# The bounds of a second weight matrix by absolute passes instead of matmuls, in a planned attention and MLP kernel whose order and engine choices are drawn anew

## The chip, the cores and the metric

The kernel runs on one core of one Trainium2 chip. The metric is the device time of one execution in microseconds, as the median of several runs. The engines are TensorE (PE, with its weight loads as PEld), VectorE (DVE), ScalarE (ACT), GpSimd (POOL) and SyncE (SP), whose queue issues all transfers.

## The reference

The kernel computes causal attention for 4 images of 12 heads, 448 positions and 64 values each, and puts the result through a dense layer, h - tanh(h), and a second dense layer.

```python
scores = scale * np.matmul(q, k.transpose(0, 1, 3, 2))
scores = np.where(mask, -1000000000.0, scores)
scores = scores - np.max(scores, axis=-1, keepdims=True)
attn = np.exp(scores)
attn = attn / (np.sum(attn, axis=-1, keepdims=True) + 1e-09)
x = np.matmul(attn, v)          # then to (4 * 448, 768)
h = x @ w_in                    # w_in: 768 x 2048, float64
out = (h - np.tanh(h)) @ w_out  # w_out: 2048 x 768, float64
```

## The kernel before

**Numbers.** Dense products run in float16 with each operand as a pair of a high and a low part, scaled by a power of two that comes from a bound on its absolute values; `split` (the high part by `scaled`, the low part on VectorE or GpSimd) makes the pairs, and a product takes three matmuls per block. The weights come as 64-bit floats. `decode` turns them into 32-bit ones: a pass on any of three engines picks three bits (the "shift" choice, written to a scratch in `e`), and for each half ScalarE scales the upper words into a PSUM bank and VectorE ors both together.

**Stages.** `first_rows` computes the first 128 positions of two images at a time in plain float32 (chunk `c` for images 0 and 1, `c2` for 2 and 3): scores, exponentials, transposes, a copy of the transposed weights out of PSUM (`pt`), and the products with v, all transposes and products through the one bank b_x. `w_in_chunk` loads, decodes, bounds and splits one eighth of w_in (8 times, two loads each). `mlp_g_first` runs the first layer for `c` and `c2`: 36 matmuls per eighth into one of the two banks b_m, a tanh on ScalarE, h - tanh on VectorE, and a split of the result. `w_out_half` loads and decodes w_out in 16 pieces of 256 rows by 384 columns, 8 per half, bounds each piece, takes the scale of the half and splits. `mlp2` is the second layer. Then `attention` runs over the four images for the other 320 positions: `prep` bounds and splits k, q and v, `weights_unit` and `weights_last` make the softmax weights and split them, a transposing transfer turns them, `values` multiplies with v and `split_x` stores x; `mlp_g` and `mlp2` follow per image. SBUF is shared over time: the g of `c` lies where the first rows were, and the pieces of w_out where w_in was decoded.

**The bounds of w_in and w_out.** `magnitudes` multiplies the two 16-bit halves of the words of a weight block in TensorE, with the block as its own stationary operand, so that the diagonal of the result holds sums of products that bound the magnitudes; 12 matmuls of 128 columns for an eighth of w_in, 6 for a piece of w_out, into the shared bank b_scales. VectorE reduces the bank, a matmul against an identity (`over_partitions`) spreads the result over the partitions, and `root_scale` takes the power of two. For q, k and v `bound` takes the largest absolute value directly: VectorE's reduction, or ScalarE's Abs with an accumulator; `bound_scale` then makes the scale.

**The order.** Nothing is written in program order. `Work.add` records each operation with its dependencies and a rank from the table RANK, `either` records alternatives on two or three engines and takes one by a letter of CFG (A, V or G), `cost` gives a duration, and `schedule` walks through a model of the engines: on the engine that is free first it takes, of the operations that are ready (or will be within AHEAD), the one of lowest rank. `emit` issues all operations by start time, so each engine has a fixed order of instructions and waits in it by semaphores. All instructions are issued by `emit`, hence one line, L288 (L302 after the change), for all.

Of the kernel before, what the change touches and what calls it, by code (L numbers as in the profile page):

```python
# [9 lines left out]
F32 = mybir.dt.float32  # L10
# [6 lines left out]
ALU = mybir.AluOpType  # L17
# [3 lines left out]
P = 128  # L21
# [4 lines left out]
class Work:  # L26
# [4 lines left out]
    LAT = {"A": 34.0, "V": 32.0, "G": 98.0, "T": 52.0, "S": 26.0}  # L31
    NEXT = {"A": 100.0, "V": 82.0, "G": 22.0}
    TURN = 94.0, 24.0
# [80 lines left out]
    def cost(self, eng, method, outs, ins):  # L114
# [11 lines left out]
        if eng == "T":  # L126
            f32 = ins[0].dtype == F32
            if method == "transpose":
                return 111.0, 170.0 if f32 else 166.0, None
            k, m = ins[0].shape[0], ins[0].shape[-1]  # L130
            quarter = ins[0].offset // ins[0].ap[0][0] if k <= 64 else None, o.offset // o.ap[0][0] if m <= 64 else None
            return (107.0 * n / P, 170.0, None) if f32 else (max(n / 2.4 + 2.5, 28.0), 166.0, quarter if min(k, m) <= 64 else None)
        if eng == "S":
            if "transpose" in method:
                c = o.size() / P
                return "turn", 1000.0 + 0.39 * c, c * 1.46
            store = o.space == bass.MemoryType.DRAM
            run = min(x.ap[-1][1] for x in ins + [o]) * size
            return ("store" if store else "load"), 450.0 if store else 440.0, o.size() * size / (360.0 if run >= 2048 else 235.0 if run >= 1024 else 385.0 if run >= 512 else 190.0)
# [14 lines left out]
        if method in ("tensor_scalar", "tensor_copy") and not psum and o.space != PSUM:  # L154
            if n < 16:
                return 142 + 5 * (n > 1) + 2.5 * n * (n > 2) + (50 if n == 1 else 65) * aps, n > 1
            return n * 0.52 + (150 if method == "tensor_copy" else 147) + 60 * aps, True
# [30 lines left out]
    def schedule(self):  # L188
# [12 lines left out]
        moved, since, last, warm, mode = 0.0, 0.0, 0.0, False, (True, True)  # L201
# [11 lines left out]
        while len(order) < n:  # L213
            t, e = min((next_at(e), e) for e in engines if ready[e] or waiting[e] or half is not None and half[1] == e)
# [3 lines left out]
            else:  # L218
# [3 lines left out]
                _, i = heapq.heappop(ready[e])  # L222
                if e == "T" and mode not in ((True, True), self.ops[i]["mode"]):
# [14 lines left out]
            if e == "T":  # L238
                turn = 0.0
                if o["mode"] != mode:  # L240
                    t, mode = max(t, free[e] + self.TURN[0]), o["mode"]
                    turn = self.TURN[1] * (mode != (True, True))
# [4 lines left out]
                warm = warm or t - since > 3100.0  # L247
                free[e] = last = t + (self.on_array(parts) + turn) * (1 if warm else 2)
                end = last + parts[-1][1] * (1 if warm else 1.15)
            elif e == "S":  # L250
                kind, issue, move = parts[0]
                moved = max(moved, t + (675.0 if kind == "turn" else 1300.0)) + move * (1.25 if t < 4500.0 else 1.0)
                free[e] = max(t + issue, moved - 2800.0)
                end = moved + {"turn": 885.0, "load": 1040.0, "store": 55.0}[kind]
            else:
# [6 lines left out]
                if part + 1 < len(parts):  # L262
                    o["start"] = t
                    free[e] = end + self.LAT[e]
# [50 lines left out]
def attention_then_mlp(ctx, tc, first, qk, v, w_in, w_out, out):  # L315
# [235 lines left out]
    def w_out_half(n):  # L551
# [4 lines left out]
        for m in range(4):  # L556
            for a in range(2):
# [405 lines left out]
```

## Time and profile before

| | us |
|---|---|
| median of 3 runs | 581.06 |
| lowest, highest | 581.05, 581.48 |
| the profiled execution | 579.8 |
| its span | 578.1 |

The span runs from the first to the last instruction; the execution's own time has 1.7 us around it. The granted clock of TensorE is 1.00 over the span. In all rows a group is named by what it writes and reads (`b_m<-slot,g`: from a weight slot and g into a bank b_m), with buffer numbers left out; `small` are the scalars per partition. An idle time in brackets or at a row's end stands with what ended it.

### The profile page before, as it was taken

What the parts mean: (1) busy time and instruction counts of PE and PEld (TensorE: products, weight loads), DVE (VectorE), ACT (ScalarE), POOL (GpSimd) and SP (SyncE); (2) the same over time, 40 slices, a digit from 0 to 9 for tenths busy, and PEclk for the clock granted to TensorE, in tenths of its full rate; (3) what the DMA queues carried; (4) which work ended last, traced back from release to release, by engine and by line L of the source; (5) the groups of instructions that cost most, each with busy time, mean ns of one, the idle gap of its engine ahead of it and who ended that gap; (6) DMA issues with size and microseconds to landing.
All of it is one profiled execution on the core that took longest, in us unless ns stands there. A gap on an engine that the chain in (4) does not pass through costs nothing.

```text
span 578.1 us, 13879 instructions
## 1 busy us (share of the span) xinstructions
PE 557.8 (96%) x5296; PEld 382.2 (66%) x5296; DVE 426.5 (74%) x1207; ACT 286.5 (50%) x751; POOL 341.9 (59%) x428
## 2 busy tenths in 40 slices
PE   6789999999999999999999999999999999999997
PEld 4567888866565666766666766566776566776664
DVE  5899999989999999699969996958599382332000
ACT  6899785744766845562555341606445150332000
POOL 3548965633563878975887888487956930542000
PEclk9999999999999999999999999999999999999999
DMA  8998379835486774365544435946123354000100
GB/s 305 343 298 310 112 213 258 239 110 178 102 161 136 183 163 78 93 174 124 119 118 92 92 66 109 211 100 125 42 69 62 69 80 101 2 1 1 28 28 27
DMA packets 109283, 74.04 MB, mean 128 GB/s; under 512 B 89760, under 2 KB 93344, under 8 KB 108704
## 3 DMA queue, kind: packets, MB, share of 16 engines
q1 hardware_dynamic: 109216, 73.15, 49.7%
q8 instruction: 41, 0.67, 0.5%
q14 instruction: 26, 0.21, 0.1%
HBM read 45.61 MB, written 5.51 MB: 88 GB/s over the span
## 4 chain that ended last, share of the span: by engine, by line
PE 68%; DVE 14%; DMA 7%; POOL 4%; issue 3%; ACT 2%; SPq 1%; DVEq 0%; POOLq 0%; ACTq 0%
PE b_m L288 57%; PE b_x L288 5%; PE b_s L288 5%; DVE pn L288 3%; DVE slot L288 2%; DVE small L288 2%; DVE prob L288 1%; PE b_scales L288 1%; DMA e<-in_v_dram 1%; DMA slot<-in_first_dram 1%; DMA g<-in_first_dram 1%; DVE g L288 1%; DVE first L288 1%; POOL first L288 1%; DMA pt<-pn 1%
## 5 line engine op out<-in xcount | busy, mean ns | idle before, releaser
L288 PE MATMUL b_m<-x,w_in 128*128 128x320 f16 (+1 forms) x1728 | 229.6, 290 | 1.6 <-DVE small L288 1.0
L288 PEld LDWEIGHTS <-w_in 128*128 128x128 f16 x1728 | 165.9, 98 | 56.3 <-issue 7.8
L288 PE MATMUL b_m<-slot,g 128*128 128x384 f16 x1152 | 191.7, 326 | 0.6 <-DVE t L288 0.5
L288 PEld LDWEIGHTS <-g 128*128 128x128 f16 x1152 | 111.1, 98 | 76.5 <-issue 5.1
L288 ACT ACTIVATE prob<-prob,small 128x256 f32<-128x256 f32 (+2 forms) x102 | 58.5, 574 | 62.2 <-DVE small L288 62.2
L288 ACT ACTIVATE t<-b_m,small 128x320 f32<-128x320 f32 (+1 forms) x70 | 37.6, 537 | 63.1 <-PE b_m L288 56.0
L288 DVE SCALAR_TENSOR_TENSOR t<-b_m,small,t 128x320 f32<-128x320 f32 (+1 forms) x70 | 39.4, 564 | 30.9 <-ACT t L288 30.7
L288 DVE CUSTOM_DVE_ANT_0 prob<-b_s,mask,small 128x384 f32<-128x384 f32 (+1 forms) x87 | 44.9, 549 | 8.6 <-PE b_s L288 7.5
L288 DVE TENSOR_SCALAR small<-small 128x1 f32<-128x1 f32 (+5 forms) x190 | 43.4, 242 | 6.1 <-ACT o L288 5.2
L288 ACT ACTIVATE o<-b_m,small 128x384 f32<-128x384 f32 x21 | 12.0, 572 | 61.3 <-PE b_m L288 61.3
L288 POOL TENSOR_SCALAR prob<-prob,small 128x384 f32<-128x384 f32 (+2 forms) x46 | 29.2, 634 | 18.9 <-ACT pn L288 6.6
L288 POOL TENSOR_SCALAR t<-t,small 128x320 f32<-128x320 f32 (+1 forms) x41 | 25.6, 625 | 23.9 <-ACT g L288 12.3
L288 POOL TENSOR_TENSOR g<-t,g 128x320 f16<-128x320 f32 (+1 forms) x40 | 34.1, 852 | 3.3
L288 PEld LDWEIGHTS <-v 128*64 128x64 f16 x1296 | 31.1, 111 | 7.1 <-issue 7.1
L288 DVE SCALAR_TENSOR_TENSOR pn<-prob,small,pn 128x256 f16<-128x256 f32 (+2 forms) x45 | 33.7, 767 | 1.5 <-ACT pn L288 0.8
L288 DVE SCALAR_TENSOR_TENSOR slot<-b_s,e 128x384 int32<-128x384 int32 x64 | 33.7, 548 | 0.9 <-POOL e L288 0.4
L288 PE MATMUL b_m<-slot,first 128*128 128x384 f16 x192 | 33.9, 326 | 0.0
L288 PE MATMUL b_s<-k,q 64*128 64x256 f16 (+2 forms) x342 | 30.6, 317 | 0.1
L288 POOL TENSOR_SCALAR g<-t,small 128x320 f16<-128x320 f32 (+1 forms) x21 | 14.5, 690 | 27.3 <-DVE t L288 25.9
L288 PEld LDWEIGHTS <-first 128*128 128x128 f16 (+2 forms) x282 | 21.7, 98 | 13.4 <-issue 2.2
L288 POOL TENSOR_TENSOR pn<-prob,pn 128x384 f16<-128x384 f32 (+2 forms) x30 | 28.0, 934 | 2.5
L288 POOL TENSOR_SCALAR e<-slot 128x768 int32<-128x768 uint16 x19 | 20.0, 1050 | 14.3 <-DMA slot<-in_moe_w_in_dram 6.6
(165 smaller groups left out, 878.8 us busy)
## 6 DMA issues: line engine op xcount, KB each, us to landing
slot<-in_moe_w_in_dram SPq DMA_DIRECT2D x16, 768.0 KB, 6.3
slot<-in_qk_dram SPq DMA_DIRECT2D x18, 384.0 KB, 3.4
slot<-in_moe_w_out_dram SPq DMA_DIRECT2D x8, 768.0 KB, 4.5
e<-in_moe_w_out_dram SPq DMA_DIRECT2D x8, 768.0 KB, 4.5
e<-in_v_dram SPq DMA_DIRECT2D x3, 1536.0 KB, 6.9
out_dram<-o SPq DMA_DIRECT2D x24, 192.0 KB, 1.9
first<-in_qk_dram SPq DMA_DIRECT2D x6, 384.0 KB, 3.7
g<-in_first_dram SPq DMA_DIRECT2D x6, 256.0 KB, 4.9
```

The costliest lines, as they stand in the source:

```text
L288: getattr(self.eng[o["eng"]], method)(*args, **kw)
```

## The change

**w_out's bounds.** In `w_out_half`, `magnitudes` and the reduction of its bank go. Each piece gets `bound` with the new meaning of the choice "b_out": ScalarE's Abs with an accumulator over 768 elements (14 pieces) or VectorE's absolute reduction (2 pieces). The scratch that the decode wrote takes the Abs pass's output, and the scale comes from `bound_scale`. Since this bound is the largest absolute value itself, the half's scale is taken from that.

**The planner.** LAT, NEXT and TURN get other numbers. SECOND is the delay between the two parts of an operation. FIRST lets GpSimd be served 25 ns earlier in ties. TensorE's costs tell array shapes apart; a turn costs the same in both directions; the clock's rise is put later; SyncE's queue is modelled deeper and its transfers with other constants; a rule "hold" is there with the value 0, which leaves it off.

**The tables.** CFG, RANK and AHEAD are drawn anew, nearly every row of them.

```diff
-    LAT = {"A": 34.0, "V": 32.0, "G": 98.0, "T": 52.0, "S": 26.0}
-    NEXT = {"A": 100.0, "V": 82.0, "G": 22.0}
-    TURN = 94.0, 24.0
+    LAT = {"A": 40.0, "V": 35.0, "G": 105.0, "T": 52.0, "S": 26.0}
+    NEXT = {"A": 94.0, "V": 80.0, "G": 12.0}
+    SECOND = 84.0
+    FIRST = 25.0
+    TURN = 94.0, 10.0
...
-            return (107.0 * n / P, 170.0, None) if f32 else (max(n / 2.4 + 2.5, 28.0), 166.0, quarter if min(k, m) <= 64 else None)
+            if f32:
+                return 107.0 * n / P + (29.0 if k <= 64 else 14.0 if m <= 64 else 0.0), 170.0, None
+            t = max(n / 2.4 + (4.2 if n == P else 2.5), 28.0) + (0.0 if m > 64 else 7.0 if k <= 64 else 0.0 if n == P else 1.5)
+            return t, 166.0, quarter if min(k, m) <= 64 else None
...
-            t, e = min((next_at(e), e) for e in engines if ready[e] or waiting[e] or half is not None and half[1] == e)
+            t, e = min((next_at(e) - self.FIRST * (e == "G"), e) for e in engines if ready[e] or waiting[e] or half is not None and half[1] == e)
+            t += self.FIRST * (e == "G")
...
-                    turn = self.TURN[1] * (mode != (True, True))
+                    turn = self.TURN[1]
...
-                warm = warm or t - since > 3100.0
+                warm = warm or t - since > 4500.0
...
-                moved = max(moved, t + (675.0 if kind == "turn" else 1300.0)) + move * (1.25 if t < 4500.0 else 1.0)
-                free[e] = max(t + issue, moved - 2800.0)
-                end = moved + {"turn": 885.0, "load": 1040.0, "store": 55.0}[kind]
+                moved = max(moved, t + (675.0 if kind == "turn" else 1000.0)) + move
+                free[e] = max(t + issue, moved - 5000.0)
+                end = moved + {"turn": 885.0, "load": 1450.0, "store": 300.0}[kind]
...
-                decode(y, t, scratch(i, 2), "_out")
-                pm = bank_1[:, 3 * P:]
-                magnitudes(pm, y, [[(k, b) for k in range(2) for b in range(3)]])
-                V.tensor_reduce(acc[:, 2 * m + a:2 * m + a + 1], pm, axis=AX.X, op=ALU.max)
+                junk = scratch(i, 2)
+                decode(y, t, junk, "_out")
+                bound(acc[:, 2 * m + a:2 * m + a + 1], y.rearrange("p a b -> p (a b)"), junk.bitcast(F32), "b_out")
...
-        root_scale(us_out[:, n:n + 1], s, a1, 0, ident16)
+        bound_scale(us_out[:, n:n + 1], s, a1, 0, mx_w)
...
-AHEAD = {"A": 85.6, "G": 32.5, "S": 149.2, "T": 1.2, "V": 93.4}
+AHEAD = {"A": 0, "G": 82.4, "S": 0, "T": 94.7, "V": 26.5, "hold": 0}
```

Of RANK, "c0" goes from -66.595 to -121.633 and "w_in" from -75.746 to -105.195 (the lower is served first). Of CFG, "p0t" (the copy of the transposed weights) goes from twelve times A to "VAAAAAAVVVVV", "k_first_lo" from "GVGGVG" to "VVVVVV", "w_in" from eight times A to "GAAGAAAA".

**What moves.** The first place is the head of SyncE's queue. `g_84` and `slot_71` to `slot_73` are where the first rows of the images lie (g_84 holds images 0 and 1), `slot_66` to `slot_68` and `slot_75` raw pieces of weights. Before:

```order
L288 DMA g_84<-in_first_dram 128x512 x3
L288 DMA g_84<-in_first_dram 128x768
L288 DMA g_84<-in_first_dram 128x512 x3
L288 DMA g_84<-in_first_dram 128x768
L288 DMA slot_66<-in_moe_w_in_dram 128x3x256
L288 DMA slot_67<-in_moe_w_in_dram 128x3x256
L288 DMA slot_68<-in_moe_w_in_dram 128x3x256
L288 DMA slot_75<-in_moe_w_out_dram 128x2x384
```

After:

```order
L302 DMA g_84<-in_first_dram 128x512 x3
L302 DMA g_84<-in_first_dram 128x768
L302 DMA slot_66<-in_moe_w_in_dram 128x3x256
L302 DMA slot_67<-in_moe_w_in_dram 128x3x256
L302 DMA slot_68<-in_moe_w_in_dram 128x3x256
L302 DMA g_84<-in_first_dram 128x512 x3
L302 DMA g_84<-in_first_dram 128x768
L302 DMA slot_71<-in_first_dram 128x512 x2
L302 DMA slot_66<-in_moe_w_in_dram 128x3x256
```

Three loads of w_in now stand between the first rows of image 0 and those of image 1.

The second place is on TensorE, where the second layer begins: `b_m_109<-slot_66,g_84` is its first product with w_out, `w_in_83` the last eighth of w_in, `slot_70` a decoded piece of w_out. Before:

```order
L288 LDWEIGHTS slot_70
L288 MATMUL b_scales<-slot_70 128x128
L288 LDWEIGHTS slot_70
L288 MATMUL b_scales<-slot_70 128x128
L288 LDWEIGHTS g_84
L288 MATMUL b_m_109<-slot_66,g_84 128x384
```

After:

```order
L302 LDWEIGHTS w_in_83
L302 MATMUL b_m_110<-x_85,w_in_83 128x256
L302 LDWEIGHTS w_in_83
L302 MATMUL b_m_110<-x_85,w_in_83 128x256
L302 LDWEIGHTS g_84
L302 MATMUL b_m_109<-slot_66,g_84 128x384
```

The bounds of a piece, six matmuls of which the last two are shown, stood right ahead of the second layer and are gone. The row numbers at which the layer begins are 1608 before and 1404 now.

The third place is VectorE while w_out is decoded: `slot_71` and `slot_72` are being decoded from `b_s_106` and `b_s_107`, `slot_66` and `slot_67` hold the split halves, `t_86` and `pn_101` are results of the first layer for `c2`. Before:

```order
L288 SCALAR_TENSOR_TENSOR t_86<-b_m_110,small_103,t_86 128x512
L288 SCALAR_TENSOR_TENSOR slot_66<-slot_67,small_103,slot_66 128x768
L288 TENSOR_REDUCE small_103<-b_scales 128x1
L288 SCALAR_TENSOR_TENSOR slot_66<-slot_67,small_103,slot_66 128x768
L288 SCALAR_TENSOR_TENSOR slot_72<-b_s_106,e_74 128x384
L288 SCALAR_TENSOR_TENSOR slot_72<-b_s_107,e_74 128x384
L288 SCALAR_TENSOR_TENSOR pn_101<-b_m_109,small_103,pn_101 128x512
L288 SCALAR_TENSOR_TENSOR slot_67<-slot_68,small_103,slot_67 128x768
L288 TENSOR_REDUCE small_103<-b_scales 128x1
```

After, on VectorE:

```order
L302 TENSOR_SCALAR e_74<-slot_75 128x768
L302 SCALAR_TENSOR_TENSOR slot_66<-slot_67,small_103,slot_66 128x768
L302 SCALAR_TENSOR_TENSOR slot_72<-b_s_106,e_74 128x384
L302 SCALAR_TENSOR_TENSOR slot_72<-b_s_107,e_74 128x384
L302 SCALAR_TENSOR_TENSOR t_86<-b_m_110,small_103,t_86 128x512
L302 SCALAR_TENSOR_TENSOR slot_66<-slot_67,small_103,slot_66 128x768
L302 SCALAR_TENSOR_TENSOR slot_72<-b_s_106,e_74 128x384
L302 SCALAR_TENSOR_TENSOR slot_72<-b_s_107,e_74 128x384
L302 SCALAR_TENSOR_TENSOR pn_101<-b_m_109,small_103,pn_101 128x512
```

and on ScalarE, where Abs passes (`e_74,small_103<-slot_70` and the like) now stand:

```order
L302 ACTIVATE e_74,small_103<-slot_70 128x768
L302 ACTIVATE b_s_106<-slot_75 128x384
L302 ACTIVATE b_s_107<-slot_75 128x384
L302 ACTIVATE pt_102<-b_m_109,small_103 128x512
L302 ACTIVATE b_s_106<-e_74 128x384
L302 ACTIVATE b_s_107<-e_74 128x384
L302 ACTIVATE slot_66<-slot_67,small_103 128x768 x2
L302 ACTIVATE e_74,small_103<-slot_71 128x768
```

VectorE's two reductions of b_scales are gone, and a decode pass on `e_74` has come to it; on ScalarE an Abs pass stands ahead of the scaling of the next piece, and one of them ahead of the tanh into `pt_102`.

## Rows read from the trace of the kernel before

**Rows 1.** The page: span, and busy us (share of the span) of each engine.
```profile
span 578.1 us, 13879 instructions
...
PE 557.8 (96%) x5296; PEld 382.2 (66%) x5296; DVE 426.5 (74%) x1207; ACT 286.5 (50%) x751; POOL 341.9 (59%) x428
```

**Rows 2.** TensorE's waits, whole span: us in total, times, longest us.
```profile
PE b_x L288 <- ACT pt L288: 4.0, 4, 2.2
```

**Rows 3.** Stretches: length, busy us by engine (instructions), granted clock, DMA share, GB/s.
```profile
0.00:10.00 10.00, 5.20 (x28) 4.34 (x28) 4.30 (x31) 5.75 (x23) 3.15 (x10) 1.00 0.80 263
10.00:20.00 10.00, 8.52 (x55) 6.27 (x55) 7.98 (x33) 8.69 (x33) 5.25 (x6) 1.00 1.04 392
0.00:60.00 60.00, 46.20 (x389) 36.34 (x390) 49.24 (x189) 49.32 (x142) 33.94 (x37) 1.00 0.86 303
60.00:123.00 63.00, 62.14 (x621) 53.68 (x618) 61.78 (x169) 43.91 (x89) 39.55 (x37) 1.00 0.65 189
0.00:212.00 212.00, 196.48 (x1892) 143.06 (x1892) 192.39 (x591) 151.90 (x392) 124.28 (x134) 1.00 0.73 210
```

**Rows 4.** The instructions on b_m over the whole span, and one of their groups.
```profile
0.00:578.10 578.10, 453.30 (x3072) 51.10 (x87) 56.38 (x101) 1.00 0.50 128
...
L288 PE MATMUL b_m<-slot,g 128*128 128x384 f16 x1152 | 191.7, 326 | 0.6 <-DVE t L288 0.5
```

**Rows 5.** TensorE's timeline in the w_out stretch: start us, us, what, count.
```profile
69.49 0.51 PE L288 MATMUL b_scales<-slot 128*128 128x128 f16 x6
69.84 3.44 PE L288 MATMUL b_m<-x,w_in 128*128 128x256 f16 x30
...
107.26 0.81 PE L288 MATMUL b_scales<-slot 128*128 128x128 f16 x6
107.91 2.13 PE L288 MATMUL b_m<-x,w_in 128*128 128x256 f16 x18
...
123.13 1.15 PE L288 MATMUL b_m<-slot,g 128*128 128x384 f16 x6
```

**Rows 6.** TensorE's timeline around a group of another array shape.
```profile
151.16 1.15 PE L288 MATMUL b_m<-slot,first 128*128 128x384 f16 x6
152.24 1.19 PE L288 MATMUL b_s<-k,q 64*64 64x448 f16 x12
```

**Rows 7.** Groups by form: count, busy us, mean ns of one, idle before.
```profile
L288 DVE SCALAR_TENSOR_TENSOR pt<-b_m,small,pt 128x512 f32<-128x512 f32 x5 | 3.7, 741 | 0.0
...
L288 DVE SCALAR_TENSOR_TENSOR k<-slot,small,k 128x448 f16<-128x448 f32 x5 | 4.8, 962 | 0.0
...
L288 DVE TENSOR_SCALAR q<-slot,small 128x320 f16<-128x320 f32 x4 | 2.8, 692 | 0.0
...
L288 DVE SCALAR_TENSOR_TENSOR pn<-prob,small,pn 128x384 f16<-128x384 f32 x16 | 12.6, 804 | 0.0
...
L288 DVE TENSOR_SCALAR e<-e 128x768 int32<-128x768 int32 x1 | 0.6, 551 | 0.0
...
L288 DVE TENSOR_SCALAR e<-slot 128x768 int32<-128x768 int32 x1 | 1.1, 1073 | 0.0
...
L288 ACT ACTIVATE e<-slot 128x768 int32<-128x768 uint16 x4 | 3.6, 909 | 1.3 <-DMA slot<-in_moe_w_out_dram 1.3
...
L288 ACT ACTIVATION_READ_ACCUMULATOR prob<-prob,small 128x1 f32 x102 | 19.1, 187 | 0.0
```

**Rows 8.** VectorE's timeline at the end of the w_out stretch.
```profile
121.19 0.28 DVE L288 TENSOR_REDUCE small<-b_scales 128x1 f32<-128x128 f32 x1
121.40 1.02 DVE L288 SCALAR_TENSOR_TENSOR slot<-b_s,e 128x384 int32<-128x384 int32 x2
122.33 0.74 DVE L288 SCALAR_TENSOR_TENSOR pt<-b_m,small,pt 128x512 f32<-128x512 f32 x1
```

**Rows 9.** Timelines of SyncE's queue and of VectorE at the start.
```profile
4.57 2.85 SPq L288 DMA_DIRECT2D slot<-in_moe_w_in_dram  x3
...
10.65 1.75 DVE L288 TENSOR_REDUCE small<-g 128x1 f32<-128x1536 f32 x1 [0.68 <-DMA g<-in_first_dram]
```

More of the change, by code (lines that the diff above doesn't have):

```diff
@@ L138, in cost @@
             run = min(x.ap[-1][1] for x in ins + [o]) * size
-            return ("store" if store else "load"), 450.0 if store else 440.0, o.size() * size / (360.0 if run >= 2048 else 235.0 if run >= 1024 else 385.0 if run >= 512 else 190.0)
+            return ("store" if store else "load"), 450.0 if store else 440.0, o.size() * size / (365.0 if run >= 2048 else 235.0 if run >= 1024 else 385.0 if run >= 512 else 190.0)
         big = [x for x in ins if per(x) > 1] if n > 1 else ins[:1]
@@ L155, in cost @@
             if n < 16:
-                return 142 + 5 * (n > 1) + 2.5 * n * (n > 2) + (50 if n == 1 else 65) * aps, n > 1
+                return 142 + 5 * (n > 1) + 2.5 * n * (n > 2) + (50 if n == 1 else 65) * aps, False
             return n * 0.52 + (150 if method == "tensor_copy" else 147) + 60 * aps, True
@@ L200, in schedule @@
         wrote = read = -1e9
-        moved, since, last, warm, mode = 0.0, 0.0, 0.0, False, (True, True)
+        moved, since, last, warm, mode = 2200.0, 0.0, 0.0, False, (True, True)
         half = None
@@ L222, in schedule @@
                 _, i = heapq.heappop(ready[e])
+                if e == "T" and mode == (True, True) != self.ops[i]["mode"] and AHEAD["hold"] and t - at[i] < AHEAD["hold"]:
+                    same = [x for x in ready[e] if self.ops[x[1]]["mode"] == mode]
+                    if same:
+                        heapq.heappush(ready[e], (self.ops[i]["rank"], i))
+                        _, i = min(same)
+                        ready[e].remove(min(same))
+                        heapq.heapify(ready[e])
                 if e == "T" and mode not in ((True, True), self.ops[i]["mode"]):
@@ L263, in schedule @@
                     o["start"] = t
-                    free[e] = end + self.LAT[e]
+                    free[e] = end + self.SECOND
                     half = free[e], e, i
@@ L930 @@
[L930 to L931 removed]
+CFG = {"early": 4, "e_bufs": 4, "b_out": "AAAAAAAAVAAAAVAA", "b_qk": "AAAAAAAVAAAAVAVVAAAAAAAAVVVVAVAVAVVAAAAVAAVAVAAV", "shift_in": "GVGGGAGGGGGGGGGG", "inverse": "VVAVAVVVVVAVAVAAAVVAAVAAVVAAVVAVVAVAVVAAVVAVAVAVAVVVAVAVVAVVVAVVVVVVAAAVVVV", "w_in": "GAAGAAAA", "w_in_lo": "VVVVVVVV", "shift_out": "GGGGGVVVVGVGGAAA", "w_out": "AAAVAAAAVAAGAAAA", "w_out_lo": "VVGVVGVVVVVVGVVV", "p0": "VGGGGGGGGGGG", "p0t": "VAAAAAAVVVVV", "x0": "AAVAAAAVAAAA", "g0": "AGAVVVGG", "g0_lo": "GGGGGGGG", "g2": "VGVVGAGV", "g2_lo": "VGVGGGGG", "g": "GGGVAAVGGAAVVGVVGAVGVAVAGAGGVAVVVGAVGGVVGGAVGGAGGAAVVAGAVVGGVGVA", "g_lo": "GGGGGGGGGGVGVVVVGGGGVVVVVVVGGVGVGGVGVGGGGGGGGGGVVVGVVVVVVGGVVGGG", "o": "AAAAVAAAAVVAVAAVVVAVVAVVAAAA", "k_first": "AAAAAA", "k_first_lo": "VVVVVV", "q_first": "AVVAVV", "q_first_lo": "VVVVVG", "v_first": "VVVAVV", "v_first_lo": "VVVVVV", "p_first": "AAAAAAAAVGAGAAAAGAAGAAVAGAGAAV", "p_first_lo": "VVVVVVGVVGVVVVVVGVGGGVGVVVGVVV", "k": "AAAAAAGVVVVVVVVAAG", "k_lo": "VVGVVVVGVGVVVVVVVG", "q": "VVGAVGGVAGVGVVVGVV", "q_lo": "GVVVVVVGGGGGGVGVGV", "v": "AVAAGVGVAGAVGVAVAA", "v_lo": "GVGGVVVVVVGGGVGVVG", "p": "GGAAVVAGVGAGGAGGAVVAAAGVGAGAGVVAVAGGGGVGVVGAAAVAGAGAAAVAGGGGGVGAAGVVVGVGAGVVAAGVAAGAGAGGGG", "p_lo": "GVVVVVVGVGVVGVVGGGGGGGGVVVGVVVVVGGVGGGGGGVVVVGVGGVVVVGVVGVGVVVVGGGGVVGGVVVGGGGGVGGGGVVGGGG", "x": "AAAAAAAAVAVAAVVAAAAVVVVA"}
@@ new lines @@
+RANK = {"c0": -121.633, "c0_load": -49.864, "c0_next": 12.036, "w_in_early": -37.897, "w_in_load": 9.073, "w_in": -105.195, "w_in_split": -67.101, "c0b": -32.545, "c0b_load": 1.137, "c0b_next": 36.206, "evac": -25.561, "evac0": -7.025, "g0": -42.201, "w_out_load": 25.5, "w_out": -13.432, "w_out_split": 14.268, "att0": -46.038, "att": -31.166, "mlp_c": 32.664, "mlp_c2": 59.783, "mlp_o": 0.546, "qk_load": 35.38, "prep": 0.623, "values": -42.924}
+AHEAD = {"A": 0, "G": 82.4, "S": 0, "T": 94.7, "V": 26.5, "hold": 0}
```

2 lines of the change are left out of this document (removed).

## The prediction

> **What bounds the kernel now.** I read the engines' shares first, then TensorE's waits, then the busy time by stretch, then single timelines. The shares [rows 1] put the matmuls at 96% of the span and VectorE at 74%. TensorE's own list of waits [rows 2] is short: its longest entry is 4.0 us. The stretches [rows 3] say where the missing time lies: in the first 60 us TensorE is busy for 46.2 us, so 13.8 us of its 20.2 us of idle time (578.1 less 557.8, rounded) fall there, and from 60 to 123 us only 0.9 us. In that second stretch VectorE has 1.2 us of idle time out of 63 as well: two engines are full side by side, and which ends last there is the question of this change.
>
> That a matmul row is busy need not mean that the array is full. The products of the two dense layers, which all land in b_m, are 3072 matmuls and fill 453.3 us [rows 4]. By the order's count they are 1152 of 320 columns, 576 of 256 and 1344 of 384, together 1,032,192 columns, and at the granted clock of 1.00, the 2.4 GHz level, these alone are 430.1 us. So 95% of that busy time is columns: TensorE is the bound, and work taken from it in a full stretch is time, if nothing else becomes late. The Trainium skill (Perfetto Trace Analysis, section Identifying the Most-Contended Engine) holds matmul busy time to be no measure of headroom and asks for the share of weight loads and the achieved FLOPs instead. By the weight loads alone (66% [rows 1]) a third of TensorE would be free and taking matmuls away would give nothing, 581.1 us; the count of columns speaks against that reading here.
>
> **Part 1: the matmuls of w_out's bounds go.** 16 pieces of w_out had six 128-column matmuls each; the order lists 96 fewer, with their 96 weight loads, and nothing takes their place (the 64 small spreads over partitions stay). A group's price is the time from its start to the next group's: 69.49 to 69.84, 0.35 us; three of the 16 took 0.65, as at 107.26 [rows 5]. 16 x 0.35 is 5.6 us; with the longer ones, and the small waits beside them, 7.2. I take 6.2, since part of a longer group is the next group's own delay.
>
> **Part 2: the turns.** Between array shapes (64-row, 64-column, full) the old order turns 139 times, the new 144, counted in the order. Six 384-column matmuls behind a 64-row group take 1.08 us to the next group [rows 6], against 6 x 0.1664 = 1.00 by the mean of 191.7 us over 1152 [rows 4]: 0.08 us a turn, 5 turns 0.4 us more. Ends: 0 and 1.
>
> **Part 3: what the bounds cost elsewhere.** 14 of the 16 go to ScalarE. The nearest rows are a 768-element pass, 909 ns, and an accumulator read, 187 ns [rows 7]: 1.0 us each with their overlap, 14 us. In the w_out stretch ScalarE has 19.1 us free of 63 [rows 3]. Each pass stands ahead of a decode and now and then ahead of a tanh on its queue, so a tanh, for which VectorE and then TensorE's second bank wait, can come up to 1.0 us late; two banks alternate, with 36 matmuls of 256 columns each, 4.1 us at the 30 in 3.44 us of [rows 5], which covers that. If ScalarE's other moves had filled its free time, each pass would be paid on the path; counted in the order at the rows' means, ScalarE's queue up to the 15th tanh gains only some 2 us in all, because copies out of PSUM and decode passes leave it. VectorE loses 16 reductions. Each held its queue for 0.21 us (121.19 to 121.40 [rows 8]): 3.4 us off.
>
> **Part 4: engine choices.** These decide it. Up to the last split of x of the first attention image (ends at 212 us), VectorE has, in the new order against the old, 6 copies of transposed weights (none before; nearest row 741 ns, a pass of the same size out of PSUM), 4 more k splits (962 ns), 5 more q passes (692 ns), 4 more weight splits of 384 (804 ns), and 4 more decode passes (551 to 1073 ns) [rows 7], less the 3.4 us: 4.4 + 3.8 + 3.5 + 3.2 + 2.2 to 4.3 - 3.4 is 13.7 to 15.8 us; all other forms together come out near nothing. These means were taken beside a busy GpSimd, and the two decode passes show the same work at half the price; as GpSimd loses 35 rows, the lower end is half, 7. I take 10. Its cover is VectorE's idle time up to 212 us, 19.6 us [rows 3], of which 5.7 fall in the first ten. Most of it I let it cover: 8.5 of the 10. It leaves 1.5 us that TensorE waits. With the cover gone it would be 10, with all of it used 0.
>
> **Part 5: the start.** SyncE's queue now has three loads of w_in between the first image and the second. They held it for 2.85 us in the old place [rows 9], and at 263 to 392 GB/s [rows 3] their 2.36 MB (3 x 128 x 768 numbers of 8 bytes) need 6 to 9 us, partly overlapping. The second image's values, whose bound opened the first split of x (its reduction started at 10.65 [rows 9]), come some 4.6 us later by that, and w_in that much earlier; VectorE gets decode work in a stretch in which it stood idle 5.7 us of 10. Both ends of c0 wait for these, so I take 0, with ends at -4.5 and +4.6. Behind 212 us I take 0 too: VectorE has a fifth of its time free there.
>
> **Sum.** 579.8 (the profiled execution) - 6.2 + 0.4 + 1.5 + 0 = 575.5. The median of the three runs, 581.06, is 1.3 above that execution, so I forecast 576.8, say **577 us**.
>
> **The rivals.** *VectorE becomes the bound (slower).* The place is the w_out stretch and the first image's attention, 60 to 212 us. If the new order leaves VectorE's idle time as it was, all but some 4 us of the upper 14 is paid by TensorE: 10 instead of my 1.5, so 577 + 8.5 = 585.5. It decides from about 6 us of uncovered work on, where it eats the whole gain of part 1. For it speaks that VectorE is 98% busy from 60 to 123 us; against it that its idle time up to 212 us is larger than what is added. *The gain is lost at the hand-over (no change).* The first product with w_out waits for a bank that VectorE frees (the pass on pt, 122.33 [rows 8], then the matmul at 123.13 [rows 5]). If the same pass ends no sooner, TensorE reaches it 6 us early and waits: 581. The work ahead of that pass on VectorE stays within 1 us of what it was, by count, which speaks for it; that VectorE had idle time to lose speaks against. *The start gets shorter too.* c0 is served ahead of w_in now; if its sixth split comes 4.5 us sooner: 572.5. That the change does not do what it says is excluded: the order shows the matmuls gone.
>
> **How the numbers follow.** Chances: forecast 0.52, VectorE the bound 0.18, lost at the hand-over 0.12, shorter start 0.18. About 0.2% (1.2 us) is what a measurement of this kernel can tell from no change, so faster means under 579.9 and slower over 582.2: faster 0.52 + 0.18 less 0.01 for its upper edge, 0.69; same 0.12; slower 0.19, the first rival and that edge. The forecast's own range, with part 1 from 5.6 to 7.2, the turns from 0 to 1 and the wait from 0 to 4, is 574 to 580. The 80% range takes in the third rival down to 571.5 and the first up to 584.5, about a tenth left out at each end.
>
> **What would show it.** In the profile after: b_scales with half its matmuls from w slots; the first product with w_out from slot_66 starting before 119 us, against 123.13; TensorE's waits on VectorE between 60 and 212 us below 3 us in sum; VectorE's idle time up to 212 us below 12 us; the last split of x of the first image no later than 212 us. I am wrong if that product starts at 122 or later, if a wait of several us on VectorE or ScalarE appears in TensorE's list, or if the first 60 us hold a TensorE idle time other than 11 to 16 us.

## The result, and the profile after

The change made the kernel slower: 586.85 us (median of 6 runs, 584.17 to 588.62) against 581.05 us of the kernel before beside it, ratio 1.0092 with a 95% interval of 1.0063 to 1.0122. The forecast was 577, the range 571.5 to 584.5. The profiled execution of the change took 587.33 us, its span is 585.6 us. All times below are medians; each run is compared with runs of the kernel before on the same chip (medians 579.9 to 581.1 us). The ratio and the interval behind a time are to those. Where the difference of two runs comes out otherwise by medians than by ratios, both are given. Three executions were disturbed (1145, 1453 and 3174 us): the ratios leave them out, and they move no median by more than 0.4 us.

The page of the change, span and busy time by engine, against [rows 1]:

```profile
span 585.6 us, 13697 instructions
...
PE 556.5 (95%) x5200; PEld 378.3 (65%) x5200; DVE 434.3 (74%) x1231; ACT 298.9 (51%) x773; POOL 315.1 (54%) x390
```

96 matmuls are gone, yet TensorE's busy time fell by 1.3 us only, and its idle time rose from 20.2 to 29.1 us. The stretches of the change (columns as in [rows 3]):

```profile
0.00:60.00 60.00, 43.59 (x357) 34.41 (x357) 51.21 (x191) 42.82 (x126) 29.42 (x32) 0.91 0.87 303
31.00:40.00 9.00, 6.99 (x43) 5.18 (x42) 8.54 (x35) 6.57 (x18) 3.86 (x5) 0.50 0.86 301
60.00:123.00 63.00, 57.67 (x519) 48.00 (x518) 60.01 (x164) 49.73 (x105) 42.62 (x41) 0.97 0.63 178
166.00:212.00 46.00, 44.56 (x543) 27.07 (x541) 44.45 (x149) 35.45 (x102) 24.30 (x30) 1.00 0.85 166
0.00:212.00 212.00, 188.31 (x1709) 135.64 (x1710) 195.98 (x591) 156.11 (x395) 112.35 (x115) 0.97 0.71 206
```

In the w_out stretch TensorE was idle for 0.9 us and is now for 5.3: the 6.2 us of matmuls were taken out and 4.4 us of waiting came in. In the first 60 us it is idle 2.6 us more. And from 31 to 40 us the granted clock is 0.50, the 1.2 GHz level. The old trace has 1.00 over the whole span, but that does not tell the pace of its first 30 us, as two rows of TensorE's timeline before show:

```profile
25.18 1.12 PE L288 MATMUL b_x<-pt,g 128*64 128x128 f32 x8 [2.23 <-ACT pt L288]
...
30.06 0.66 PE L288 MATMUL b_x<-pt,g 128*64 128x128 f32 x8
```

So both kernels start at the slower pace. The old one leaves it 2.3 us ahead of its first dense matmul, the change for good only behind that.

TensorE's longest waits, whole span, against [rows 2] (us in total, times, longest):

```profile
PE b_s L302 <- DMA g<-in_first_dram: 5.0, 2, 3.5
PE b_scales L302 <- DVE small L302: 3.5, 8, 1.0
PE b_x L302 <- DVE x L302: 3.4, 3, 1.5
PE b_x L302 <- DVE small L302: 2.9, 2, 1.5
PE b_x L302 <- DVE pt L302: 1.9, 2, 1.8
```

No entry is large, but VectorE stands in four of the five. TensorE's timeline, at the places that the prediction named:

```profile
14.81 1.22 PE L302 MATMUL b_s<-g 64*128 64x128 f32 x8 [1.47 <-DMA g<-in_first_dram]
...
38.92 1.49 PE L302 MATMUL b_m<-x,w_in 128*128 128x256 f16 x6
...
76.79 0.63 PE L302 MATMUL b_x<-ident,pn 128*128 128x128 f32 x4 [1.52 <-DVE x L302]
...
78.84 1.12 PE L302 MATMUL b_x<-pt,slot 128*64 128x128 f32 x8
...
126.99 5.04 PE L302 MATMUL b_m<-slot,g 128*128 128x384 f16 x30 [0.35 <-DVE pt L302]
```

The second image's scores wait for its load. The first product with w_in starts at 38.92 us; in the trace before it is this row:

```profile
32.37 0.82 PE L288 MATMUL b_m<-x,w_in 128*128 128x256 f16 x6
```

At 76.79 TensorE waits 1.5 us for VectorE. Behind that the clock falls in this execution (the eight products at 78.84 us take 1.12 us, not 0.66). The granted 0.82 and 0.84 from 75 to 80 and 80 to 85 us make that an estimated 1.7 us; the profiled executions of three runs below in the order of the change (neither bound, matmuls back, copies back) have 1.00 in the w_out stretch. The first product with w_out comes at 126.99 us instead of 123.13 [rows 5]. Two of the three signs that the prediction set for being wrong are there: that product behind 122 us, and 16.4 us of TensorE's idle time in the first 60. The third, a wait of several us on VectorE or ScalarE, is there only as a sum (3.5 us in 8 waits of at most 1.0).

### The profile page after: what moved, and what is told of

It is laid out like the page before. It is cut to its first block, busy times and chain, and to the rows that moved or that the text cites. A ratio compares the mean times of both kernels' runs of the same rounds, so it can differ in the third digit from the quotient of the medians.

```text
span 585.6 us, 13697 instructions
## 1 busy us (share of the span) xinstructions
PE 556.5 (95%) x5200; PEld 378.3 (65%) x5200; DVE 434.3 (74%) x1231; ACT 298.9 (51%) x773; POOL 315.1 (54%) x390
## 4 chain that ended last, share of the span: by engine, by line
PE 38%; DVE 7%; issue 3%; DMA 2%; POOL 1%; ACT 0%; POOLq 0%; ACTq 0%; DVEq 0%
PE b_m L302 35%; PE b_x L302 2%; DVE small L302 2%; DVE prob L302 1%; PE b_s L302 1%; DMA e<-in_v_dram 1%; DVE first L302 1%; DVE pn L302 1%; DVE g L302 1%; DVE t L302 0%; DVE x L302 0%; DVE k L302 0%; DMA pt<-pn 0%; DVE v L302 0%; POOL v L302 0%
## 5 line engine op out<-in xcount | busy, mean ns | idle before, releaser
L302 PEld LDWEIGHTS <-w_in 128*128 128x128 f16 x1728 | 167.7, 98 | 57.2 <-issue 7.5
L302 ACT ACTIVATE o<-b_m,small 128x384 f32<-128x384 f32 x17 | 9.7, 573 | 76.8 <-PE b_m L302 76.8
L302 POOL TENSOR_SCALAR prob<-prob,small 128x384 f32<-128x384 f32 (+2 forms) x47 | 32.0, 682 | 27.9 <-ACT pn L302 22.9
L302 DVE TENSOR_SCALAR small<-small 128x1 f32<-128x1 f32 (+5 forms) x205 | 41.6, 220 | 3.5 <-ACT prob L302 1.4
L302 POOL TENSOR_SCALAR t<-t,small 128x320 f32<-128x320 f32 (+1 forms) x43 | 27.4, 638 | 18.5 <-DVE g L302 8.3
L302 DVE SCALAR_TENSOR_TENSOR pn<-prob,small,pn 128x384 f16<-128x384 f32 (+2 forms) x46 | 30.0, 668 | 2.3 <-ACT pn L302 1.3
L302 POOL TENSOR_SCALAR pn<-prob,small 128x256 f16<-128x256 f32 (+2 forms) x23 | 17.2, 751 | 24.9 <-DVE small L302 9.1
L302 POOL TENSOR_SCALAR e<-slot 128x768 int32<-128x768 uint16 x18 | 18.7, 1039 | 18.1 <-DMA slot<-in_moe_w_in_dram 14.1
```

Source lines behind the costliest of these rows:

```text
L302: getattr(self.eng[o["eng"]], method)(*args, **kw)
```

## The experiments

To change one thing and leave the rest, I wrote the planner's answer out: a list of operation numbers and an engine letter for each, of the kernel before or of the change. "Planned time" is the planner's own start of an operation; it only serves to choose operations.

```diff
-        for i in self.schedule():
+        for i in ORDER:
             o = self.ops[i]
+            o["eng"] = ENGINE[i]
```

### What the edit of the bounds is worth

**Edit alone.** ORDER and ENGINE of the kernel before; only `w_out_half` as in the change.

> Every engine's order and every engine choice of the kernel before, word for word, with only the bounds of w_out exchanged: the six matmuls and the reduction of a piece go, an absolute pass on ScalarE stands in their place (VectorE takes the last piece). If the edit is worth what part 1 and part 3 of the prediction say (5.6 to 7.2 us of matmuls off the path, ScalarE's 15 us covered), this runs at 574 to 577 us. If the freed time only turns into waits at the hand-over to the second layer, or the passes on ScalarE delay decode and tanh, it runs at 580 to 582.

588.65 us, ratio 1.0137 (1.0099 to 1.0176): 8 us *slower* than the same order with the matmuls. Its w_out stretch:

```profile
60.00:123.00 63.00, 54.25 (x498) 45.45 (x496) 54.12 (x147) 53.22 (x113) 39.21 (x36) 1.00 0.65 189
```

TensorE is idle for 8.8 us, VectorE for 8.9 us (before: 0.9 and 1.2), ScalarE is busy for 53 of 63: no engine is full any more. How that comes about at one place is seen on ScalarE's timeline of this run

```profile
78.21 0.83 ACT L303 ACTIVATE e<-slot 128x768 f32<-128x768 f32 x1
78.94 0.19 ACT L303 ACTIVATION_READ_ACCUMULATOR e<-slot 128x1 f32 x1
79.04 0.57 ACT L303 ACTIVATE pt<-b_x 128x512 f32<-128x512 f32 x1
```

and on TensorE's:

```profile
79.66 0.66 PE L303 MATMUL b_x<-pt,slot 128*64 128x128 f32 x8 [1.38 <-ACT pt L303]
```

An absolute pass stands ahead of the copy of the transposed weights; TensorE waits 1.38 us for the copy. In the kernel before the same matmuls started at 78.72 us without a wait.

**No bounds.** Same order, matmuls and passes both gone.

```diff
-                bound(acc[:, 2 * m + a:2 * m + a + 1], y.rearrange("p a b -> p (a b)"), junk.bitcast(F32), "b_out")
+                bound(acc[:, 2 * m + a:2 * m + a + 1], y[:, 0, :2], junk.bitcast(F32)[:, :2], "b_out")
```

> The order and the engines of the kernel before, without the six matmuls of a piece and without the absolute passes: VectorE takes the bound of a piece from 2 of its 768 columns, where its reduction of the bank stood (this leaves the rest of the bound out). It prices the matmuls alone. If TensorE is the bound of the w_out stretch, as the prediction held, 5.6 to 7.2 us come off the time of the kernel before (580.3 with these runs): 573 to 575. If the decode of w_out through ScalarE, VectorE and GpSimd sets the end of that stretch, TensorE only waits in place of the matmuls: 579 to 581, and the first product with w_out stays within 1 us of 123.13 us.

581.29 us, ratio 1.0011 (0.9994 to 1.0028): the matmuls taken away, with only a short pass on VectorE in place of its reduction, are worth nothing. Two of its stretches, and the first product with w_out on TensorE's timeline:

```profile
60.00:123.00 63.00, 58.22 (x532) 48.62 (x531) 59.90 (x174) 43.80 (x89) 40.70 (x40) 1.00 0.68 196
166.00:212.00 46.00, 44.39 (x542) 26.89 (x537) 41.59 (x140) 32.25 (x99) 29.45 (x38) 1.00 0.83 161
```

```profile
121.14 1.15 PE L303 MATMUL b_m<-slot,g 128*128 128x384 f16 x6 [1.55 <-DVE small L303]
```

3.9 of the 6.2 us are waits in the same stretch. The second layer begins 2.0 us earlier (not within 1 us, as expected if the decode alone set the end). Of these 2.0 us, 0.5 is left where VectorE's last low part of x of the first image ends, at 212.36 us against 212.89, and nothing at the end.

**Idle passes.** The same, with 15 absolute passes back on ScalarE, into a column that nothing reads.

```diff
+            if i < 0:
+                o, y, f, acc = self.passes[-1 - i]
+                self.nc.scalar.activation(o, y, f, accum_out=acc)
+                continue
```

> The run without bounds (581.29 us; each piece's bound from 2 columns on VectorE) with the first 15 absolute passes put back on ScalarE in the places where the run with the edit alone had them, but into a column that nothing reads, their output to a place of its own. Theory of ScalarE's queue: as the run with the edit alone, 586 to 589. If the cost comes from the half's scale and the splits behind it waiting for the last pass: 581 to 583.

587.86 us, ratio 1.0132 (1.0099 to 1.0166). So the passes cost 6.6 us (7.0 by the ratios) by their place in ScalarE's queue alone; nobody waits for their results. The path of it is in VectorE's list of waits from 60 to 123 us. Without passes:

```profile
DVE first L303 <- ACT first L303: 0.8, 1, 0.8
DVE slot L303 <- ACT b_s L303: 0.2, 1, 0.2
```

and with the idle ones:

```profile
DVE first L307 <- ACT first L307: 2.6, 2, 1.4
DVE x L307 <- ACT x L307: 2.2, 3, 1.0
DVE slot L307 <- ACT b_s L307: 1.8, 3, 0.7
```

With two smaller entries VectorE waits for ScalarE for 7.6 us in that stretch instead of 1.0 (8.3 with the edit alone, 0.8 in the kernel before). TensorE's waits for the copies on ScalarE rise far less, from 4.6 to 5.3 us over the whole span. The 6.6 us more of waiting are as long as the loss, which speaks for a delay that went mostly through VectorE: the high halves of splits (`first`, `x`) and decode scalings (`b_s`) reached it late from ScalarE, and it had only 3.1 us of idle time in the stretch.

**Junk apart.** A rival cause was the scratch that pass and decode share.

```diff
-y.rearrange("p a b -> p (a b)"), junk.bitcast(F32), "b_out")
+y.rearrange("p a b -> p (a b)"), v16_block[:, 8 * P:14 * P], "b_out")
```

> As the run with the edit alone (588.65 us), but the absolute passes write their output to a place of its own (a part of the block for v that is not in use before 139 us of planned time) and no longer into the scratch of the decode. Theory of the scratch: the decode of the next piece but one may only begin when the absolute pass has read and written, so each pass lengthens the chain load, decode, bound; without that the time falls to 581 or lower. Theory of ScalarE's queue: the passes cost because they stand ahead of decode scalings, copies of transposed weights and tanh in the queue, so the time stays at 586 to 589.

588.79 us, ratio 1.0131 (1.0107 to 1.0155), as the edit alone: the scratch is not it. The same edit in the change:

> The change with the same single edit: its absolute passes write to a place of their own. Theory of the scratch: below 584. Theory of ScalarE's queue: 585 to 588, as the change itself (586.85).

584.73 us, ratio 1.0077 (1.0053 to 1.0101): between the two ranges, and not to be told from the change.

**The edit in the new order.** Once the matmuls put back into the order of the change, once neither matmuls nor passes (the edit of the run without bounds).

> The order and the engines of the change, written out, with the old bounds of w_out put back: six matmuls where the absolute pass was started, the reduction on VectorE 0.85 us behind in planned time. If the edit pays in the new order as well, this is 5.6 to 7.2 us longer than the change (586.9), 592 to 594. If the new order makes TensorE wait for VectorE in that stretch anyhow, the matmuls fall into waits and it stays at 586 to 589.

588.93 us, ratio 1.0124 (1.0083 to 1.0166), some 2 us above the change, with overlapping intervals.

> The order and the engines of the change without its absolute passes: each bound is taken from 2 of the 768 columns on VectorE (this leaves the rest of the bound out), 0.85 us of planned time behind where the pass began. If the passes on ScalarE cost in the new order what they cost in the old (6.6 us): 579 to 582. If the new order has room for them: 585 to 588, and the loss lies in the order itself.

584.56 us, ratio 1.0084 (1.0066 to 1.0102): the passes cost some 0.5 us by the ratios and 2.3 by the medians here. The new order has room for them: in the change VectorE's list from 60 to 123 us has no wait for ScalarE. But even without any bound it is 0.8% behind the old order *with* its matmuls. The rest of the loss lies in the order.

### Where the new order loses

**Two starts.** The operations that the kernel before starts in its first 60 us of planned time (S), in either order, then the rest in the other:

```python
ORDER = [i for i in before if i in S] + [i for i in change if i not in S]   # old start
ORDER = [i for i in change if i in S] + [i for i in before if i not in S]   # new start
```

> The operations that the kernel before starts in its first 60 us of planned time (424 or fewer of 2731) in its order and on its engines, everything else in the order and on the engines of the change. Theory of the start (the later second image leaves TensorE idle and its clock falls back to the lower level from 30 to 41 us, so the first dense matmul starts at 38.92 us instead of 32.37): 586.9 less about 6.5 us, 579 to 581, and the granted clock is 1.00 over the first 60 us. Theory of the later order (new engine choices fill VectorE from 60 to 212 us, and TensorE waits there): little comes back, 584 to 587.

583.97 us, ratio 1.0063 (1.0037 to 1.0090); the first dense matmul is at 32.24 us. 1.7 us come back by the ratios, 2.9 by the medians. (The granted clock is 0.89 over the first 60 us, not 1.00 as expected, and that matmul is not later for it.)

> The other half: those same early operations in the order and on the engines of the change, everything else as in the run with the edit alone. Theory of the start: 6.5 us longer than the run with the edit alone, about 581 to 583, with the first dense matmul near 39 us. Theory of the later order: within 2 us of the run with the edit alone, 575 to 578.

592.54 us, ratio 1.0211 (1.0172 to 1.0250): 3.9 us above the edit alone (4.3 by the ratios). By both, the start of the change costs 2 to 4 us, and the 6.5 us that the first dense matmul comes later are regained in part.

**The load order.** The kernel before with one move on SyncE's queue:

```diff
 first rows of image 0, 4 loads
+w_in, 3 loads
 first rows of image 1, 4 loads
-w_in, 3 loads
```

> The kernel before, order and engines word for word and with its matmul bounds, except that on SyncE's queue the first three loads of w_in stand ahead of the second image's first rows, as in the change. Part 5 of the prediction put the two ends of this at -4.5 and +4.6. Theory that the late image alone makes the start longer: 583 to 585, the first dense matmul 3 us or more behind 32.37 us. Theory that the start is lost by the new choices of engines and the new order of the other engines: 579 to 581.5.

586.46 us, ratio 1.0111 (1.0086 to 1.0136): 6 us from this alone. TensorE's timeline and VectorE's reduction of the second image:

```profile
15.02 1.23 PE L289 MATMUL b_s<-g 64*128 64x128 f32 x8 [4.68 <-DMA g<-in_first_dram]
...
38.97 0.82 PE L289 MATMUL b_m<-x,w_in 128*128 128x256 f16 x6
```

```profile
17.25 1.75 DVE L289 TENSOR_REDUCE small<-g 128x1 f32<-128x1536 f32 x1 [7.29 <-DMA g<-in_first_dram]
```

The reduction starts 6.6 us later than in [rows 9], and the first dense matmul stands at 38.97 us, where the change has it too (38.92). The opposite move in the change:

> The change with one thing moved: on SyncE's queue the second image's first rows stand ahead of the first three loads of w_in again. Theory of the late image: the first dense matmul moves from 38.92 us towards 33 us and 3 to 6 us come off the change's 586.85: 581 to 584. Rival, the other engines of the change are ordered around the late image (decode of w_in stands ahead of the first image's softmax on VectorE), so the loads alone give nothing back: 586 to 589.

588.08 us, ratio 1.0137 (1.0106 to 1.0169): nothing comes back. Its VectorE shows why:

```profile
14.02 0.56 DVE L303 SCALAR_TENSOR_TENSOR slot<-b_s,e 128x384 int32<-128x384 int32 x1 [5.12 <-POOL e L303]
14.50 0.68 DVE L303 COPY pt<-b_x 128x512 f32<-128x512 f32 x1
```

and TensorE:

```profile
15.23 1.12 PE L303 MATMUL b_x<-pt,g 128*64 128x128 f32 x8 [4.57 <-DVE pt L303]
```

The decode of w_in stands ahead of the copy on VectorE's queue, and w_in is now late: TensorE waits 4.57 us for the copy. The queues fit the load order that they were made for.

**Copies.** `p0t` from twelve times A to "VAAAAAAVVVVV" and the two letters of `p0`, in the kernel before:

> The kernel before with only the letters of two choices in the first rows exchanged for those of the change, in their places: six of the twelve copies of transposed weights go from ScalarE to VectorE, the first normalisation goes to VectorE and the last to GpSimd. Part 4 charged these 4.4 us to VectorE, covered by its idle time. If they are covered: 579.5 to 581.5. If VectorE is full from 60 to 123 us and TensorE waits for it: 583 to 585.

582.60 us, ratio 1.0049 (1.0027 to 1.0071): 2 to 3 us, and a new wait in TensorE's list:

```profile
PE b_x L289 <- DVE pt L289: 2.1, 2, 1.4
```

The reverse in the change, alone and together with the early image:

> The change with the six copies of transposed weights back on ScalarE and the two exchanged normalisations on their old engines, in their places. In the old order this exchange cost 2 us. If VectorE's queue is what makes it cost: 584 to 585.5. If ScalarE, which now has the absolute passes too, holds them up as long: 586 to 589.

> The change with both: second image's rows first, copies on ScalarE. If both theories hold and add up: 579 to 582, no longer to be told from the kernel before, perhaps below it. If either falls: as the better of the two runs beside it.

585.94 us, ratio 1.0096 (1.0071 to 1.0121), and 589.74 us, ratio 1.0158 (1.0126 to 1.0191). Neither undoes the loss, and the two together are slower than either alone. In the first, the waits for copies on ScalarE rise from 1.6 to 2.9 us, on the queue that has the absolute passes too.

**VectorE's load.** The old start with five decode passes moved from VectorE to GpSimd (`shift_out`, pieces 5 to 8 and 10: V to G):

> As the run with the old start and everything else of the change (583.97 us), but the five decode passes of w_out's pieces that the change gave to VectorE go to GpSimd, in their places. VectorE is rid of some 4 us in the stretch from 60 to 123 us, where it has 2.9 us idle of 63. Theory that VectorE is the bound there: 2 to 4 us come off, 580 to 582. If the chain decode, bound, scale, split through ScalarE and GpSimd is what TensorE waits for, GpSimd's longer pass changes nothing or costs: 584 to 586.

586.72 us, ratio 1.0106 (1.0079 to 1.0132): slower by 2.8 us, though VectorE is busy for 56.8 us of the 63 instead of 60.1. Less work on VectorE does not shorten the stretch when GpSimd has to do it; what VectorE's load costs by itself is not shown.

**The clock.** 94 idle matmuls ahead of nine waits of the change:

```diff
             o["eng"] = ENGINE[i]
+            for _ in range(FILL.get(i, 0)):
+                self.nc.tensor.matmul(*self.junk, start=True, stop=True)
```

> The change, with 94 matmuls of 128 columns without use put on TensorE ahead of the nine groups of the first 38 us for which it waits (12, 12, 8, 4, 14, 8, 12, 16 and 8 of them); nothing reads what they write. Theory of the clock: TensorE's pauses keep it at the lower level up to 41 us; kept busy it runs at the higher level from about 20 us on, the groups of the first images take half the time (0.63 us for four transposes, 0.71 us for eight score products) and 2 to 4 us come off: 583 to 585. Rival, the start is set by loads, decode and softmax on the other engines and TensorE's pace does not matter there: 586 to 588.

586.78 us, ratio 1.0091 (1.0067 to 1.0114): no change. The fillers did raise the clock early, as these rows show (1.09 us for four transposes at the lower level):

```profile
22.72 0.63 PE L305 MATMUL b_x<-ident,pn 128*128 128x128 f32 x4
...
34.99 1.05 PE L303 MATMUL b_scales<-ident 128*128 128x128 bf16 x16 [1.43 <-DVE small L305]
35.88 0.61 PE L305 MATMUL b_x<-ident,pn 128*128 128x128 f32 x4
...
39.77 0.82 PE L305 MATMUL b_m<-x,w_in 128*128 128x256 f16 x6
```

Yet the first dense matmul is no earlier. That alone does not settle it: the fillers at 34.99 us wait for VectorE themselves and then stand ahead of the transposes, which start at 35.88 us instead of 33.96, so they take back what the faster pace gives. Two things on record say more. The run with the matmuls back has the change's start; its groups keep the slower pace throughout (1.12 us for the eight products at 29.25 us, 0.66 at 29.20 in the change), and its first dense matmul is at 38.23 us, not later than 38.92. And of 84 executions of the kernel before, the 48 with a mean granted clock of 0.999 or 1.00 have a median of 579.8 us, the other 36 of 581.0; of the six of the change, the three at 0.999 or 1.00 took 584.2 to 586.4 us, the others 587.3 to 588.6. So a fall of the clock goes with 1 to 2 us, and most of the loss is there without it. (That mean shows falls and not the slow pace of the start, which both kernels have; what this costs is not shown.)

**Two that settle little.** A splice that takes only the stretch before the second layer from the change, and the kernel before with five decode passes of w_out moved from ScalarE to GpSimd:

> Old start (operations before 60 us of planned time), then the operations that the change starts before its first product with w_out, in its order and on its engines, and behind that the order and engines of the kernel before (the last two bounds of w_out among them). If the stretch from 60 to 123 us only gives back what the edit saves and the rest of the loss (3.7 us from 580.3 to 583.97) lies in the first image's attention and behind it, where the change chose other engines: 579.5 to 581.5. If the loss is made before 123 us: 583 to 585.

> The kernel before, its matmul bounds and its order, with the five decode passes of w_out that ScalarE has between 67 and 108 us of planned time put on GpSimd in their places. ScalarE's queue is rid of 4.5 us in the stretch in which 15 us more cost 6.6. If that queue paces the stretch, some 2 us come off: 577.5 to 579. If GpSimd's place in the decode is what paces it (moving VectorE's passes there cost 2.8 us): 582 to 585.

588.52 us, ratio 1.0148 (1.0118 to 1.0177), and 582.43 us, ratio 1.0053 (1.0032 to 1.0075). In the first, TensorE waits 8.6 us for VectorE's small results (4.7 us or less in the runs that it is joined from): the joint itself makes waits, and what share the first image's attention has in the loss stays open. The second was an attempt to gain from a lighter ScalarE, and it loses 2.5 to 3 us; the cause was not followed up. No version ran faster than the kernel before.

## Why the prediction was wrong

**Part 1 failed, by its whole size.** "16 x 0.35 ... I take 6.2" priced the matmuls about rightly (TensorE's busy time falls by 5.4 us in the run without bounds) and put them on the path wrongly. The argument was that TensorE is the bound since its busy time is 95% columns. But in the old order these matmuls lie where TensorE would else wait: without them the time is 581.29, not 574. The text had the fact in hand: VectorE has 1.2 us idle beside TensorE's 0.9 in that stretch. With two engines full side by side, taking the work from one of them here only turned it into waiting. The other reading, which the prediction weighed by the Trainium skill (Perfetto Trace Analysis, section Identifying the Most-Contended Engine: busy matmul time does not tell headroom) and set aside, would have given 581.1. The run without bounds agrees with that time. It shows waits, on VectorE above all, in the place of the matmuls, and nothing of the weight loads.

**Part 2** (turns, +0.4) is too small to show; no run tests it.

**Part 3 was wrong for the order it was read from.** "1.0 us each ... covered": the passes took what was said (0.83 and 0.19 us), but 15 us on a queue with 19.1 us free cost 6.6 us, with no one waiting for their results. The cover was reckoned for the tanh and its two banks; what came late were high halves of splits and decode scalings, for which VectorE waited (7.6 us instead of 1.0), and in part the copies of transposed weights through the one bank b_x. In the order of the change, which was planned with the passes, they cost 0.5 to 2.3 us.

**Part 4 had the right place and the right amount of work, and the wrong cover.** Up to the end of the last low part of x of the first image VectorE has these rows (columns as in [rows 3]) before, in the change, and in the run with the old start:

```profile
0.00:212.89 212.89, 197.37 (x1898) 143.60 (x1899) 193.28 (x594) 152.57 (x394) 125.08 (x135) 1.00 0.73 210
...
0.00:219.08 219.08, 195.39 (x1808) 140.49 (x1809) 202.77 (x613) 161.87 (x411) 114.99 (x120) 0.97 0.71 203
...
0.00:216.42 216.42, 191.58 (x1808) 137.87 (x1809) 197.08 (x603) 163.85 (x419) 117.27 (x122) 0.97 0.73 206
```

VectorE is busy for 9.5 us more in the change, against the 10 that I took. But its idle time falls only from 19.6 to 16.3 us: it covers 3.3 us, not 8.5, and that pass ends 6.2 us later. In the run with the old start it covers nearly nothing (19.3 us idle, 3.8 us more work, 3.5 us later). This is a count and not a cause: with the late image alone, in the old order, the same pass is 6.6 us late with 0.7 us more work. TensorE is idle from 60 to 212 us for 7.3 us against 1.7. The wait at 76.79 us comes from this order on VectorE:

```profile
73.44 2.81 DVE L302 SCALAR_TENSOR_TENSOR w_in<-slot,small,w_in 128x1536 f16<-128x1536 f32 x1
76.17 0.47 DVE L302 SCALAR_TENSOR_TENSOR x<-b_x,small,x 128x256 f16<-128x256 f32 x1
```

A long split of w_in stands ahead of the short pass that frees b_x. The copies alone, 4.4 us in my sum, cost 2 to 3 us in the old order; the run with the old start and all else of the change is 3.7 us slower than the kernel before although it has the edit. Which of its choices make these 3.7 us is not shown.

**Part 5 failed too.** "I take 0, with ends at -4.5 and +4.6": the late image alone costs 6 us in the old order, more than the upper end, since the second image's reduction came 6.6 us later and not 4.6, a figure that no row gave. In the change, whose queues expect it, the start costs 2 to 4.

**The sum.** The -6.2 did not come, and a loss came on top: 1.7 to 2.9 us for the start (the change less the run with the old start) and 3.7 for all else (that run less the kernel before, the passes and what is left of the matmuls among it). These two make up the whole loss by the way they are formed; they divide it and do not explain it.

**The rivals.** The time of the first rival, 585.5, is nearest. Its condition, that the new order leaves VectorE's idle time as it was, holds in the run with the old start and in part in the change. That VectorE's amount of work is the reason is not shown: what is seen at 76.79 us is a short pass behind a long one, and with less work on VectorE (five decode passes moved to GpSimd) the time was longer. The first rival also leaves out the start. The hand-over (0.12) is what the run without bounds did in its time, in the old order, though the second layer began 2.0 us earlier there. The shorter start went the other way.

**What was to be seen:** b_scales has 96 matmuls from w slots, half, as said. The first product came at 126.99, not before 119. Waits on VectorE from 60 to 212 us are 5.8 us, not below 3. VectorE's idle time up to 212 us is 16.0 us, not below 12. The last low part of x of the first image ran at 218.60 us, not by 212 us (212.41 before). All but the first speak against the forecast.

## What to carry to other kernels

Work on a busy engine is worth its time only if that engine's queue alone sets the end: where two engines are full side by side, price a removal first by a run that leaves the work out and puts next to nothing in its place. Free time on an in-order queue need not cover an added pass; ask which short, awaited instruction the pass will stand ahead of. A planned order belongs to its load order and engine letters as one thing: a part put back alone, even the better one, can cost more than it returns.

## What the runs showed of the hardware

A split of w_in on VectorE took 1.80 to 1.94 us in the kernel before, but 2.35 to 2.81 us four times in the change. In the row at 73.44 us above, GpSimd's timeline of the change has

```profile
73.48 1.16 POOL L302 TENSOR_TENSOR g<-t,g 128x512 f16<-128x512 f32 x1
74.72 2.26 POOL L302 TENSOR_SCALAR e<-slot 128x768 int32<-128x768 uint16 x1
```

VectorE's 2.81 us is its usual 1.8 and nearly the 1.16 of the GpSimd pass beside it; GpSimd's next pass, mostly 0.9 us elsewhere, took 2.26 and ended 0.7 us behind VectorE's split. In the kernel before such splits meet GpSimd passes too, and there GpSimd's pass is the longer one (2.11 us at 50.62 us, 0.69 for the other of its shape). The Trainium skill (SBUF — State Buffer, section SBUF: two separate sides) says that these two engines share a pair of ports under an exclusive lock, for a VectorE pass with two SBUF inputs; the rows agree. Here one such meeting held the pass that frees b_x back by 1 us, and TensorE behind it.

The granted clock reads 1.00 in the first 30 us of the trace before, and up to 41 us in the run with the matmuls back, although groups take nearly twice as long there as later (1.12 and 0.66 us for eight products of one shape); the pace of a group tells more than that column. In the change the pace rose at 27.57 us (0.63 us for four transposes) and fell again with 0.50 granted from 31 to 40 us, after pauses of 0.7 and 1.0 us on TensorE ahead of the groups at 27.57 and 29.20 us; in the run with the matmuls back, with the same start and pauses of 0.7 us at these places, it had not risen there.
